# An attention-and-FFT kernel on one core: the order of every operation, the PSUM banks and the filler matmuls from tables instead of a scheduler

## The chip, the cores and the metric

One core of a Trainium2 chip. The metric is the time of one execution on the device in microseconds (us). Each run also records the span of the core (first to last instruction, about 1.8 us less than the metric) and the mean granted clock of TensorE (PE), 1.000 being full speed. A few more words: a PSUM bank is where a matmul of this program puts its result (`psA`, `psB`, `pvb` and `bg` below); a fall is a stretch in the middle of the kernel in which the granted clock is half of full (0.50 from 192.1 to 202.3 us in the profile of before); the head is the time until the first exponentials run at their regular pace, the tail what follows the last of them. Comparisons are between runs of the same call on the same chip where this is said.

A word on states: a run is called slow if it lies over 1.5% above the fastest of its kernel.

## The reference

A sigmoid gate mixes two branches of the same input x (2048 tokens, 448 features, bf16): attention with 16 heads of 28, and a filter in the frequency domain.

```python
def reference(A_x, A_wqkv, A_wo, B_x, B_w_r, B_w_i, gate_w):
    x = A_x
    g = _sigmoid((x * gate_w).sum(-1, keepdims=True))
    a = _A_ref(x, A_wqkv, A_wo)      # softmax(q k^T / sqrt(28)) v, then @ wo
    b = _B_ref(x, B_w_r, B_w_i)      # irfft2(rfft2(x) * (w_r + 1j * w_i))
    return g * a + (1 - g) * b
```

## The kernel before

The kernel describes 3123 operations, each with engine, duration, dependencies and a priority key. A list scheduler on the host puts them in order; the program then keeps that order on each engine. The work in the steady state is a chain of *score steps*: PE computes the scores of three 128x512 tiles into `psA`, or of two into `psB`, in turn; ScalarE (ACT) exponentiates them into `ring`; PE multiplies the exponentials with the values into `pvb`. A further share of exponentials is made on VectorE (DVE) from scores in one of two `bg` banks. Everything of the FFT branch is squeezed in between, also through the two `bg` banks.

The profile prints rows*columns with each: 128*128 for a projection, 32*128 for a score. A head has 28 features, padded to 32, so a score uses 32 rows, and the tiles of one step sit on different row groups; they run side by side (in the profile of before, three take 0.40 us together at 186.99, two 0.39 at 185.90, and a lone one 0.37 at 186.13):

```python
            def fm(st=st, slot=slot):
                for i in range(2):
                    for e, (n, kt, s) in enumerate(st):            # 2 or 3 tiles
                        ...
                            self.mm(slot[:, e, o:o + w], self.k[g][32 * s:32 * s + 32, ...],
                                    self.q[g][32 * s:32 * s + 32, ...], True, True,
                                    tile_position=(32 * s, 0))     # 32 rows of the array
            m = sc.op("PE", 0.23, fm, deps, -1000 + i * .001, 0.0, "row", name="score")
```

The scheduler already had fillers, matmuls of zeros with no purpose but to keep PE active. It decided on them by PE's *busy time* in the last 3.4 us:

```python
HAMW, HAMF = 3.4, 0.6838
...
        def share(t):
            a = t - HAMW
            while pebusy and pebusy[0][1] <= a:
                pebusy.pop(0)
            return sum(e - max(s, a) for s, e in pebusy) / HAMW

        def fill(t):
            ...
            if n < 96 or (share(t) >= HAMF and not head):
                return False
            ...
            o = Op("PE", n / 2400.0, lambda: self.filler(target, n), (), 0.0, 0.0, "col", ...)
```

## Time and profile before

| | before |
|---|---|
| time, 3 runs (4 with the later one) | 414.34, 415.25, 417.07 (415.83) us |
| profiled execution | 417.67 us, span 415.9, clock 0.973 |
| ACT busy / PE busy | 94% / 95% of the span |
| exponentials of three banks | 170, start to start 2.23 to 2.24 us where nothing disturbs |
| same, summed over what exceeds 2.24 | 16.7 us |

How to read it: ACT's sequence of exponentials is the spine (52% of the chain that ended last). As long as each exponential of three banks starts 2.24 us after the last one, nothing else in the kernel matters. So the useful question is not who is busy, but where that interval grows, and what was late there. The lines themselves stand in the prediction.

### The profile page before, as it was taken

What the parts mean: (1) busy time and instruction counts of PE and PEld (TensorE: products, weight loads), DVE (VectorE), ACT (ScalarE), POOL (GpSimd) and SP (SyncE); (2) the same over time, 40 slices, a digit from 0 to 9 for tenths busy, and PEclk for the clock granted to TensorE, in tenths of its full rate; (3) what the DMA queues carried; (4) which work ended last, traced back from release to release, by engine and by line L of the source; (5) the groups of instructions that cost most, each with busy time, mean ns of one, the idle gap of its engine ahead of it and who ended that gap; (6) DMA issues with size and microseconds to landing.
All of it is one profiled execution on the core that took longest, in us unless ns stands there. A gap on an engine that the chain in (4) does not pass through costs nothing.

```text
span 415.9 us, 12556 instructions
## 1 busy us (share of the span) xinstructions
PE 393.7 (95%) x5361; PEld 150.2 (36%) x5361; DVE 365.4 (88%) x629; ACT 392.0 (94%) x358; POOL 45.7 (11%) x95
## 2 busy tenths in 40 slices
PE   6998999999999999999999999999999999999995
PEld 4543333333433333234342332423334333333333
DVE  5758989888799999998699998798999989999965
ACT  4899999999999999998898998999999999999992
POOL 5400501001040000001041000000500000010000
PEclk9999999999999999997798996999999999999999
DMA  8500010001032310300103000231401200010102
GB/s 221 141 2 3 2 41 5 2 2 51 25 86 64 103 45 2 82 4 6 43 2 85 2 3 9 58 116 38 119 13 55 78 28 2 13 32 7 37 26 78
DMA packets 26548, 18.00 MB, mean 43 GB/s; under 512 B 10704, under 2 KB 24956, under 8 KB 26492
## 3 DMA queue, kind: packets, MB, share of 16 engines
q1 hardware_dynamic: 25660, 16.94, 14.9%
q8 instruction: 42, 0.69, 0.7%
q10 hardware_dynamic: 832, 0.26, 0.3%
q14 instruction: 14, 0.11, 0.1%
HBM read 11.31 MB, written 1.84 MB: 32 GB/s over the span
## 4 chain that ended last, share of the span: by engine, by line
ACT 53%; PE 28%; DVE 10%; issue 7%; DMA 2%; ACTq 0%; DVEq 0%
ACT ring L1620 52%; PE bg L908 11%; PE pvb L908 7%; PE psA L908 5%; PE psB L908 4%; DVE y L1574 3%; DVE pd L1584 2%; DMA U<-Y 1%; DMA U<-in_A_wqkv_dram 1%; DVE xtok L2003 1%; DVE k L1306 1%; DVE xtok L1316 0%; DVE pvs L1733 0%; DVE q L1306 0%; DVE xtok L2037 0%
## 5 line engine op out<-in xcount | busy, mean ns | idle before, releaser
L1620 ACT ACTIVATE ring<-psA 128x1536 bf16<-128x1536 f32 x170 | 260.9, 1535 | 6.4 <-PE psA L908 3.1
L1620 ACT ACTIVATE ring<-psB 128x1024 bf16<-128x1024 f32 (+1 forms) x170 | 188.0, 1106 | 3.8 <-PE psB L908 2.7
L1574 DVE TENSOR_SCALAR y<-bg 128x512 uint16<-128x512 f32 x176 | 117.3, 682 | 10.7 <-PE bg L908 10.0
L1584 DVE TENSOR_SCALAR pd<-y 128x2048 uint16<-128x2048 uint16 x176 | 118.6, 693 | 0.8
L908 PEld LDWEIGHTS <-k 32*128 32x128 bf16 (+1 forms) x1064 | 40.7, 91 | 125.8 <-issue 121.2
L908 PE MATMUL pvb<-ring,vw 128*32 128x512 bf16 (+1 forms) x872 | 78.0, 386 | 0.7 <-DVE pvs L1733 0.4
L908 PE MATMUL psA<-q,k 32*128 32x512 bf16 (+1 forms) x525 | 68.4, 383 | 5.1 <-ACT ring L1620 3.8
L908 PE MATMUL bg<-q,k 32*128 32x512 bf16 x176 | 65.2, 383 | 4.2 <-DVE Y L1958 1.6
L908 PE MATMUL psB<-q,k 32*128 32x512 bf16 (+1 forms) x347 | 67.5, 385 | 1.6 <-ACT ring L1620 1.4
L908 PE MATMUL pvb<-pd,vd 128*32 128x512 bf16 x704 | 64.5, 391 | 1.2 <-DVE pd L1584 0.8
L908 PEld LDWEIGHTS <-vw 128*32 128x32 bf16 x872 | 20.9, 95 | 33.3 <-issue 29.2
L908 PEld LDWEIGHTS <-vd 128*32 128x32 bf16 x704 | 18.4, 95 | 27.7 <-issue 22.9
L1478 POOL TENSOR_SCALAR vd<-vf 128x348 bf16<-128x348 f32 x16 | 20.6, 1290 | 60.7 <-DVE vf L1467 22.4
L1738 POOL CAST rhl<-rr 128x16 bf16<-128x16 f32 x15 | 6.0, 399 | 188.4 <-DVE rr L1737 188.4
L908 PEld LDWEIGHTS <-xT 128*128 128x128 bf16 (+3 forms) x512 | 21.2, 99 | 12.7 <-issue 9.6
L1958 DVE CAST Y<-bg 128x450 bf16<-128x450 f32 x32 | 19.6, 618 | 2.5 <-PE bg L908 1.2
L908 PE MATMUL bg<-xT,wpk 128*32 128x512 bf16 (+2 forms) x244 | 18.7, 389 | 0.0
L908 PE MATMUL bg<-xT,wpq 128*32 128x512 bf16 (+1 forms) x240 | 18.0, 383 | 0.2 <-DVE k L1306 0.2
L908 PE MATMUL bg<-Bd,xT 128*32 128x450 bf16 (+1 forms) x256 | 17.3, 356 | 0.0
L908 PE MATMUL bg<-wo,q 128*32 128x448 bf16 x236 | 16.4, 355 | 0.0
L908 PE MATMUL bg<-Bd,xtok 113*32 113x448 bf16 x240 | 16.0, 355 | 0.0
L1306 DVE TENSOR_SCALAR k<-bg 128x512 bf16<-128x512 f32 x15 | 10.3, 687 | 5.6 <-PE bg L908 5.4
(130 smaller groups left out, 316.6 us busy)
## 6 DMA issues: line engine op xcount, KB each, us to landing
U<-Y SPq DMA_DIRECT2D x32, 112.5 KB
CR<-cRB SPq DMA_DIRECT2D x8, 256.0 KB
out_dram<-U SPq DMA_DIRECT2D x14, 112.0 KB
CR<-cCS SPq DMA_DIRECT2D x8, 192.0 KB
xtok<-in_A_x_dram SPq DMA_DIRECT2D x3, 448.0 KB
xT<-escr SPq DMA_DIRECT2D x2, 512.0 KB
Wg<-in_B_w_r_dram SPq DMA_DIRECT2D x8, 112.5 KB
Wg<-in_B_w_i_dram SPq DMA_DIRECT2D x8, 112.5 KB
```

The lines of the kernel that those rows point to most:

```text
L908: self.pin(self.nc.tensor.matmul(out, lhsT=lhsT, rhs=rhs, start=start, stop=stop, **kw))
L1306: self.pin(nc.vector.tensor_scalar(out=dst, in0=self.bgi(it), scalar1=SQ, scalar2=None, op0=ALU.mult))
L1478: self.pin(nc.gpsimd.tensor_scalar(out=self.vd[g][:, f, :, :, 0:DH + 1], in0=self.vf[:], scalar1=PHGAIN[f], scalar2=None, op0=ALU.mult))
L1574: self.pin(nc.vector.tensor_scalar(out=ys[:, s, :], in0=self.bgi(it), scalar1=127 * UNITS, scalar2=0.0, op0=ALU.add, op1=ALU.max))
L1584: self.pin(nc.vector.tensor_scalar(out=fl(pds).bitcast(U16), in0=fl(ys), scalar1=float(PHASE[f]), scalar2=0.25, op0=ALU.add, op1=ALU.mult))
L1620: self.pin(nc.scalar.activation(out=self.ring[:, u0:u0 + len(st), :], in_=slot[:, 0:len(st), :], func=ACT.Exp, scale=LN2 / UNITS))
L1738: b = self.pool(0.3, lambda: self.pin(nc.gpsimd.tensor_copy(out=rhl[:, 0, :], in_=rr[:])), (a,), kk)
L1958: self.pin(nc.vector.tensor_copy(out=y[:], in_=self.bgi(it)[:, 0:F2]))
L2003: self.pin(nc.vector.tensor_tensor(out=t4.rearrange("p (a b) f -> p a b f", a=2), in0=free_dims(self.bgi(it), [[0, 2], [F, 2], [1, F]]), i ...
```

## The change

The intent, from the code: the order of every operation and the bank of every user of the two `bg` banks come from tables that were searched beforehand, so the scheduler goes. Fillers are in a table, too. The code also gives each PE operation a weight `util`, by which a score counts 0.23 per tile and not 1; this program sets it and never reads it, so that the search which made the table used it is my inference.

```diff
-HAMW, HAMF = 3.4, 0.6838
+HAMW, HAMF = 3.4, 0.6803
...
-KOFF = ( ...                        # 280 lines of priority offsets (cut)
+ORDER = (
+    119, 1, 0, 2, 7, 3, 12, 22, 94, 4, 21, 13, 32, 6, 10, 20, 14, 27, 5, 91, 8, 25, 11, 130, 2690, 19, 98, 18, 96,
+    ...                             # 3123 numbers (cut)
+FILLS = (                           # position, columns, target
+    (117, 192, 0), (126, 256, 1), (144, 256, 0), (144, 160, 0), (545, 128, 8), (834, 256, 8), (969, 256, 8),
+    ...                             # 51 entries (cut)
+BANKS = (
+    "0100011110110011010011111111111000011101010100101111010110011000100101100010101100011110010100110001"
+    ...
-    def run(self, nbg_tiles, dunits, dfree):      # the list scheduler (cut)
+    def run(self):
+        ...
+        for p, i in enumerate(ORDER):
+            while j < len(FILLS) and FILLS[j][0] == p:
+                n, t = FILLS[j][1:]
+                ...                  # a filler of n columns into bank t
+            o = self.ops[i]
+            assert all(d in done for d in o.deps)
+            done.add(o)
+            order.append(o)
...
+            m.util = 0.23 * len(st)                # a score of len(st) tiles
```

## The prediction

> **What bounds the kernel now.** I read the shares of the engines and the slices first, then the chain that ended last, then what ScalarE (ACT) waited for, then stretches of 4 us, then single instructions.

> The page of the kernel before (busy time by engine, the slices, the chain):

> ```profile
> span 415.9 us, 12556 instructions
> PE 393.7 (95%) x5361; PEld 150.2 (36%) x5361; DVE 365.4 (88%) x629; ACT 392.0 (94%) x358; POOL 45.7 (11%) x95
> ...
> PEclk9999999999999999997798996999999999999999
> ...
> ACT 53%; PE 28%; DVE 10%; issue 7%; DMA 2%; ACTq 0%; DVEq 0%
> ```

> ACT is 94% busy and more than half of the chain is its exponential (ring). PE looks equally full. The clock row is the odd one: five slices between 190 and 260 us ran below full clock. Which waits of ACT are real (waits of ACT alone):

> ```profile
> ACT t L1832 <- PE psA L908: 5.0, 1, 5.0
> ACT ring L1620 <- PE psA L908: 3.1, 5, 1.2
> ACT ring L1620 <- PE psB L908: 3.1, 5, 0.9
> ACT ring L1620 <- PE bg L908: 2.4, 5, 0.8
> ```

> The 5.0 is the tail. The exponential waits only for PE. Where: stretches of 4 us (busy us of each engine, then granted clock):

> ```profile
> 184.00:188.00 4.00, 3.69 (x56) 1.34 (x51) 4.00 (x8) 4.00 (x5) 0.00 (x0) 1.00 0.02 6
> 188.00:192.00 4.00, 3.24 (x37) 0.98 (x33) 4.00 (x7) 4.00 (x5) 1.17 (x2) 1.00 0.02 7
> 192.00:196.00 4.00, 3.93 (x34) 1.87 (x31) 3.40 (x7) 3.33 (x4) 0.75 (x2) 0.51 0.02 3
> 196.00:200.00 4.00, 4.00 (x37) 2.01 (x38) 1.74 (x3) 2.48 (x3) 0.00 (x0) 0.50 0.39 98
> 200.00:204.00 4.00, 4.00 (x49) 1.09 (x41) 1.90 (x3) 3.02 (x3) 0.00 (x0) 0.71 0.05 15
> ```

> A thin stretch on PE (37 matmuls, where 56 is usual) is followed by half clock for about 10 us, and ACT loses its full use there. The same around 219 us in the timelines of ACT and of PE:

> ```profile
> 214.27 1.48 ACT L1620 ACTIVATE ring<-psA 128x1536 bf16<-128x1536 f32 x1
> 216.51 1.51 ACT L1620 ACTIVATE ring<-psA 128x1536 bf16<-128x1536 f32 x1
> 218.74 1.53 ACT L1620 ACTIVATE ring<-psA 128x1536 bf16<-128x1536 f32 x1
> 221.99 1.45 ACT L1620 ACTIVATE ring<-psA 128x1536 bf16<-128x1536 f32 x1
> ```
> ```profile
> 218.60 0.37 PE L908 MATMUL bg<-q,k 32*128 32x512 bf16 x1
> 218.90 0.40 PE L908 MATMUL pvb<-ring,vw 128*32 128x512 bf16 x4
> 219.42 0.62 PE L908 MATMUL pvb<-pd,vd 128*32 128x512 bf16 x4
> 219.80 0.67 PE L908 MATMUL pvb<-ring,vw 128*32 128x512 bf16 x4
> 220.40 0.60 PE L908 MATMUL psB<-q,k 32*128 32x512 bf16 x2
> ```

> Starts of one exponential of three banks to the next: 2.23 or 2.24 us undisturbed, then 3.25. The same shape of matmul goes from 0.40 to 0.62 us near 219.4.

> From the first exponential of three banks (9.97) to the last (405.22) ACT takes 395.25 us for 169 intervals; at 2.24 each that is 378.6. The excess of 16.7 us I split by interval:
> - clock: 192.20 to 202.99 is 3 intervals, 10.79 - 6.72 = 4.07; 218.74 to 224.84 is 2, 6.10 - 4.48 = 1.62; 254.32 to 261.07 is 2, 6.75 - 4.48 = 2.27. Together **7.96 us**.
> - head, 9.97 to 18.50, 3 intervals: 1.81.
> - two long intervals at full clock: from 91.39 (3.46) and from 288.13 (3.23): 1.22 + 0.99 = 2.21.
> - the rest, 4.7, lies in many small ones: short exponentials of the weights w in the same queue, and waits of 0.1 to 0.3.

> [...] the clock falls near 192.15, 219.45 and 253.6, which are 8.0 and 10.0 windows apart, and the low stretches last about 3, 1 and 2 windows. [...] between 188 and 192 PE was busy 3.24 of 4 us, and no idle of PE there exceeded 0.45 us. [...] Counting every matmul as its columns[...] times the share of rows and of columns of the array that it uses, the whole run uses 0.61 of the array, but the windows ahead of the three falls only 0.40, 0.30 and 0.36. The lowest windows on that grid that did not fall were 0.38 to 0.39. So the limit appears to lie between 0.36 and 0.40, my boundaries being sure to 0.2 us; this is my estimate. A score of two or three 32-row tiles uses 2/4 or 3/4 of the array for its time, and a lone score into bg 1/4: thin stretches consist of these.

> **The change, part by part.**
> 1. *Host code.* The scheduler becomes a table. No instruction comes of that. Both programs have the same 3123 operations with the same work; ACT's order is nearly untouched (18 of 361 moved), so the sum of ACT's work stays.
> 2. *Fillers.* 24 become 51; each is four loads and four matmuls of zeros, so PE has 216 instruction rows more. By their columns they take 2.25 us before and 4.57 after: +2.3 us of array time. PE has 22 us of idle in the span, and they are put where PE has little to do; on the path I count 0.3.
> 3. *Order.* I cut each PE order at its scores and took windows of three score steps (3 x 1.12 = 3.36 us at the undisturbed pace). Of 325 windows beyond the head, before has 13 under 0.40 of array use, 5 under 0.35, minimum 0.30. After has 1 under 0.40 (0.394), none under 0.35. The mean is nearly equal (0.64 and 0.65): work was levelled, not added. [...] most of the 7.96 us goes: I count -7.7, leaving 0.3 for one chance in ten or so of a fall of 2 to 3 us.
> 4. *The long pairs.* PE's own work from one score of three tiles to the next (scores into bg taken as concurrent) had one case over 2.24 us: 3.10 at steps 72 and 73, which is the 1.22 us lost at 91.39. After, the largest is 2.47, at step 306. So -1.2 + 0.25, about -0.9.
> 5. *More mode changes.* Changes between row-tiled and column-tiled matmuls on PE go from 649 to 692. At an estimated 0.1 us (the difference between PE's idle of about 0.2 us in such places and none within a mode) that is 4 us of PE's slack; on the path I count 0.5.
> 6. *Banks.* 181 of 361 users of the two bg banks change bank. An item then waits for another reader, but both banks are read by the same DVE: 0 in the mean.
> 7. *The head.* PE has 53 operations before its first score where it had 46, which would start ACT some 0.5 us later; fewer stand between later scores (the fifth step has 1.41 us of work where it had 2.40, and 18.50 is just where ACT waited 1.2 us). I set both against each other: 0. The DMA order changes much: the bulk of wv moves from the 5th issue of the SyncE queue to the 23rd. By sizes some 3.4 MB stand before it, and the stretch from 0 to 13 us moved 236 GB/s, 3.07 MB, with 300 and more near its end, so it lands at about 15 us (estimate); its first user ran at 15.72. Just in time.

> Sum for the span: 415.9 - 7.7 - 0.9 + 0.3 + 0.5 = 408.1. The profiled execution took 417.67 as the metric has it, 1.77 more than its span, so 409.9. The timed runs (median 415.25) were faster than the profiled one, but they carry falls of the clock as well: with none, the profiled one would be at 409.7. I also give the 0.99 lost at 288 an even chance to vanish: **409.4 us**, 1.4% less.

> **Rivals.**
> - *The clock is not what it seems.* If the falls came by something else than array use, such as the DMA bursts, the new order would keep them: 414 to 417. Against: DMA is at 0.02 before the fall at 192, and all three falls follow thin windows. For: windows at 0.38 and 0.39 did not fall, so the limit is not seen sharply.
> - *PE becomes the bound.* The fillers and mode changes make 6 us more of PE time against 22 us idle. If they land next to scores, ACT waits 0.1 more at many of the 170 pairs, up to 5 us: 412 to 414. Against: apart from one pair no pair of steps holds more than 2.1 us of PE work.
> - *The head pays.* If wv or the weights behind it land 2 us late, the in-order PE queue holds the next score back: 411 to 412.
> - *More comes back.* If levelling removes the small waits as well (4.7 us in many places), 406 to 407.

> **Range and chances.** The centre needs the clock gain and nothing worse; both the second and third rival are one-sided upward, the fourth reaches 406.5. Range 406.8 to 412.8. Faster by over 2% means under 406.9: only if the small waits go too, 0.11. Slower by over 2% needs over 423.5, for which nothing in the profile stands: 0.01. Within 2%: 0.88.

> **What would show it.** Right: a clock row of nines, mean granted clock near 1.0 outside the last slice, no stretch where the matmul of 0.40 us becomes 0.61; ACT's 3.25 to 4.00 intervals gone; intervals of 2.24 unchanged; PE busy time up in count by 108 matmuls, but its idle near 20 us. Step 4: no interval of 3.4 us near the step of 91 us. Step 7: the fourth exponential of three banks near 18 us, no wait for wv. Wrong: a clock below 1.0 in any slice but the last; an interval of ACT stretched to 2.4 and more at many places with PE named (rival two); ACT waiting over 2 us before 20 us, PE held by a DMA (rival three).

The sum: 415.9 - 7.7 - 0.9 + 0.3 + 0.5 = 408.1 for the span, and 409.4 for the time. What is under the -7.7 is the count of stretches under 0.40 (13 before, 1 after); that they bring the falls was the estimate from three falls. The "windows" are stretches of 3.41 us: in the clock records of the trace of before all seven changes lie a whole number of 3.413 us apart (55, 3, 5, 1, 9, 2 and 45). Columns are counted at the kernel's own 2400 per us (the trace of e4 has 448 columns every 0.189 us, 2370 per us). The 0.1 us for a change of mode is in the trace of before, too: between 30 and 185 us, where a score (32*128) follows a column-tiled matmul (128*32) or the reverse, PE starts the second 0.10 us later than the columns of the first would have it (median of 238 places).

## More of the kernel before

At the very start 14 matmuls of zeros run before any data is there:

```python
        for i in range(14):
            self.pe(256, lambda: self.mm(self.psA[:, 2, 0:256], self.zero[:, 0:P], self.zero[:], True, True),
                    (ms["zero"],), K0 + i * .01, dur=0.214)
```

## The result, and the profile after

After: 410.46, 411.44, 411.45 and 412.0 us, median **411.44**; before in the same rounds 414.34, 415.25, 415.83 and 417.07, median 415.54. Ratios in this text are the mean time of one kernel's fast runs over that of the other's of the same rounds, so not quite the ratio of the medians: here 0.9897, with a 95% interval of 0.9859 to 0.9935. That is 1% faster, within the 2% that counts as the same, and inside the predicted range, but 2 us above the predicted 409.4.

The page of the kernel after (span, busy time, granted clock in 40 slices, shares of the chain):

```profile
span 409.6 us, 12755 instructions
...
PE 392.5 (96%) x5469; PEld 152.3 (37%) x5469; DVE 365.9 (89%) x629; ACT 389.8 (95%) x358; POOL 41.9 (10%) x95
...
PEclk9999999999999999999999999999999999999999
...
ACT 53%; PE 34%; issue 8%; DVE 2%; POOL 1%; DMA 1%; ACTq 0%; DVEq 0%; POOLq 0%
```

The row of the clock has only nines: the four low slices of before (7, 7, 8 and 6; the prediction says five) are gone. What ACT waited for in the kernel after (us in total, times, longest):

```profile
ACT t L1498 <- PE psA L572: 5.2, 1, 5.2
ACT wpq L691 <- POOL wpq L671: 2.8, 1, 2.8
ACT ring L1286 <- PE psB L572: 2.5, 3, 1.9
...
ACT ring L1286 <- PE psA L572: 0.4, 1, 0.4
```

In the kernel before, exponentials waited 8.6 us in 15 pieces for `psA`, `psB` and `bg`. Now it is 2.9 us in 4 pieces, and 1.9 of that is one wait, that of the very first exponential. The stretches of 4 us that held the first fall of the clock, in the kernel after (busy us of each engine, granted clock, share of the DMA engines, GB/s):

```profile
188.00:192.00 4.00, 3.91 (x56) 1.39 (x52) 4.00 (x7) 4.00 (x5) 0.00 (x0) 1.00 0.03 6
192.00:196.00 4.00, 3.75 (x58) 2.43 (x51) 4.00 (x8) 4.00 (x4) 0.00 (x0) 1.00 0.00 0
196.00:200.00 4.00, 4.00 (x61) 1.48 (x62) 3.97 (x7) 4.00 (x5) 0.00 (x0) 1.00 0.34 87
```

From 188 to 192 PE started 37 matmuls before and starts 56 now; its busy time was 3.24 us and is 3.91. The clock stays at 1.00 and ACT stays full.

The balance over the span, by starts of the exponentials of three banks (excess means time over 2.24 us per interval):

| part | before | after | difference |
|---|---|---|---|
| until the first one starts | 9.97 | 13.72 | +3.75 |
| excess, first 20 us | 1.88 | 0.54 | -1.34 |
| excess, 20 to 190 us | 3.39 | 2.67 | -0.72 |
| excess, 190 to 265 us (the falls) | 8.50 | 0.87 | -7.63 |
| excess, after 265 us | 2.92 | 2.14 | -0.78 |
| from the last one to the end | 10.68 | 11.10 | +0.42 |
| span | 415.9 | 409.6 | -6.3 |

The rows of excess are rounded separately and agree with the spans to 0.05 us. So 9.1 us were gained between 20 us and the last exponential, and about 2.4 lost at the head. These are two single executions, and that of before was an unusually slow one; between the medians of the timed runs the gain is 4.1 us. Where? First the exponentials in ACT's timeline, before:

```profile
9.97 1.45 ACT L1620 ACTIVATE ring<-psA 128x1536 bf16<-128x1536 f32 x1 [0.43 <-PE psB L908]
...
18.50 1.45 ACT L1620 ACTIVATE ring<-psA 128x1536 bf16<-128x1536 f32 x1 [1.20 <-PE psA L908]
```

and after:

```profile
13.72 1.45 ACT L1286 ACTIVATE ring<-psA 128x1536 bf16<-128x1536 f32 x1 [1.89 <-PE psB L572]
...
20.98 1.49 ACT L1286 ACTIVATE ring<-psA 128x1536 bf16<-128x1536 f32 x1
```

The fourth is 2.5 us late, and so is the eleventh (36.95 against 34.46). PE's timeline in the head, before:

```profile
6.83 0.60 PE L908 MATMUL psA<-xT,wpk 128*128 128x256 bf16 x4
```

and after:

```profile
4.53 0.84 PE L572 MATMUL psA<-zero 128*128 128x256 bf16 x3
7.47 0.40 PE L572 MATMUL psB<-xT,wpq 128*128 128x256 bf16 x1 [2.10 <-ACT wpq L688]
7.65 1.06 PE L572 MATMUL psA<-xT,wpk 128*128 128x256 bf16 x4
```

The same four matmuls took 0.60 us before and take 1.06 after. They keep that pace until about 12.5 us. PE is at half clock there, although the row of the clock shows a nine in these slices: in the packed trace of this run the first record of the clock begins at 12.7 us, where the clock rises (at 4.3 us in the kernel before), and the row and the mean count the time ahead of it as full. Reading durations of one shape is the surer way. Beside this, PE stood idle from 5.4 to 7.5 us: only ten of the 14 matmuls of zeros come before the projections in the new order (two of the other four run at 11.92 and 15.72 us, behind the projections, which waited 2.10 us for the weights), and a 448 KB load moved ahead of a part of the weights.

### The profile page after: what moved, and what is told of

It reads as the page before. It is cut to its first block, busy times and chain, and to the rows that moved or that the text cites. A ratio compares the mean times of both kernels' runs of the same rounds, so it can differ in the third digit from the quotient of the medians.

```text
span 409.6 us, 12755 instructions
## 1 busy us (share of the span) xinstructions
PE 392.5 (96%) x5469; PEld 152.3 (37%) x5469; DVE 365.9 (89%) x629; ACT 389.8 (95%) x358; POOL 41.9 (10%) x95
## 4 chain that ended last, share of the span: by engine, by line
ACT 53%; PE 34%; issue 8%; DVE 2%; POOL 1%; DMA 1%; ACTq 0%; DVEq 0%; POOLq 0%
ACT ring L1286 53%; PE bg L572 14%; PE pvb L572 9%; PE psA L572 6%; PE psB L572 5%; DVE y L1239 1%; DMA CR<-cRB 1%; PE bg L581 0%; POOL wpq L671 0%; POOL vd L875 0%; POOL wo L880 0%; DVE pd L1249 0%; ACT w L1068 0%; ACT t L1498 0%; DVE pvs L1399 0%
## 5 line engine op out<-in xcount | busy, mean ns | idle before, releaser
L1286 ACT ACTIVATE ring<-psA 128x1536 bf16<-128x1536 f32 x170 | 266.1, 1566 | 2.7 <-PE psB L572 1.9
L1286 ACT ACTIVATE ring<-psB 128x1024 bf16<-128x1024 f32 (+1 forms) x170 | 193.2, 1136 | 0.6 <-PE psB L572 0.6
L572 PEld LDWEIGHTS <-k 32*128 32x128 bf16 (+1 forms) x1064 | 44.0, 91 | 116.9 <-issue 110.3
L572 PE MATMUL pvb<-ring,vw 128*32 128x512 bf16 (+1 forms) x872 | 75.4, 377 | 0.3 <-DVE pvs L1399 0.2
L572 PE MATMUL pvb<-pd,vd 128*32 128x512 bf16 x704 | 63.2, 384 | 0.0
L572 PEld LDWEIGHTS <-vd 128*32 128x32 bf16 x704 | 16.7, 94 | 27.6 <-issue 23.8
L1404 POOL CAST rhl<-rr 128x16 bf16<-128x16 f32 x15 | 4.0, 267 | 223.9 <-DVE rr L1403 223.9
L572 PEld LDWEIGHTS <-xT 128*128 128x128 bf16 (+3 forms) x512 | 19.3, 96 | 12.7 <-issue 10.1
L1142 POOL TENSOR_SCALAR vd<-vf 128x348 bf16<-128x348 f32 x16 | 19.5, 1222 | 33.4 <-DVE vf L1131 32.6
L572 PE MATMUL bg<-wo,q 128*32 128x448 bf16 x236 | 16.7, 355 | 0.0
L572 PE MATMUL bg<-X,R 128*32 128x225 bf16 (+1 forms) x288 | 14.3, 294 | 0.0
```

Source lines behind the costliest of these rows:

```text
L572: self.pin(self.nc.tensor.matmul(out, lhsT=lhsT, rhs=rhs, start=start, stop=stop, **kw))
L1142: self.pin(nc.gpsimd.tensor_scalar(out=self.vd[g][:, f, :, :, 0:DH + 1], in0=self.vf[:], scalar1=PHGAIN[f], scalar2=None, op0=ALU.mult))
L1286: self.pin(nc.scalar.activation(out=self.ring[:, u0:u0 + len(st), :], in_=slot[:, 0:len(st), :], func=ACT.Exp, scale=LN2 / UNITS))
L1404: b = self.pool(0.3, lambda: self.pin(nc.gpsimd.tensor_copy(out=rhl[:, 0, :], in_=rr[:])), (a,), kk)
```

## The experiments

Their labels e1 to e11 follow the order in which they ran.

The theories after the result. *One:* the falls in the middle come from windows in which too few **rows** of the array are active, and the new order and fillers remove them. Rival: PE's busy time or its idle gaps decide. *Two:* the head is late because the clock has not risen yet. Rival: it is late because data land late and more work stands before the first score.

### Without the fillers (e1), and fillers on a quarter of the rows (e2)

```diff
 FILLS = (
-    ... 47 entries beyond the tenth score step
+    # only the first four, in the head
```

> The kernel after without its 47 fillers beyond the tenth score step; order and banks as they are. Counted from the order, the three-step windows under 0.40 of array use go from 1 to 4 (minimum 0.28), where before had 13 and fell 3 times. Theory (order does most, the fillers close the last holes): 0 to 2 falls of the clock in the profile, near steps 243 to 245 or 263 if any, mean granted clock 0.98 to 1.00, 411 to 414 us. Rival (the fillers carry the gain): three or more falls, clock under 0.98, 414 to 417 us. Rival (fillers only cost PE time): faster than after by 0.5 us or more at a clock of 1.00.

```diff
-    def filler(self, bank, n):
+    def filler(self, bank, n, quarter):          # quarter: beyond the head
+        r = 32 if quarter else P
...
-            self.mc(self.bgt[bank][:, 0:n], self.zero[:, 0:P], self.zero[:, 0:n], True, True)
+            self.mc(self.bgt[bank][:, 0:n], self.zero[0:r, 0:P], self.zero[0:r, 0:n], True, True)
```

> The same 47 fillers kept, each as long as before (same columns, same four column tiles), but on 32 rows in place of 128: a quarter of the array. Theory (the clock follows the share of the array in use): falls where the run without fillers has them, time within 1 us of it. Rival (the clock follows PE's busy time, whatever the share): as the kernel after, 411.4 us, clock 0.994 to 1.00. If the run without fillers shows no fall, this one cannot tell the two apart.

Measured: e1 had 410.44, 411.65, 415.38 and 417.16 us, with clocks of 0.997, 0.993, 0.981 and 0.982; ratio to before 0.9971 (0.9889 to 1.0052). e2 had 411.36 to 413.7, median 412.92, with clocks of 0.998 to 1.000 in all four; ratio 0.9977 (0.9921 to 1.0032). The kernel before, on the same chip, had a median of 414.47, at clocks of 0.976 to 0.994.

What follows: without fillers two of four runs fell by some 5 us; the other two are as fast as the changed kernel. In the profiled run of e1, which did not fall, the excess over 2.24 us is 6.21; in the changed kernel it is 6.22. So the 47 fillers cost nothing on the path, and the order alone does not seem enough: two of four runs fell, against three of 32 with all the fillers (counted below), which points that way and does not settle it. e2 is inconclusive: by theory one its fillers should have helped less, yet no run fell. Its three runs without a profile took 412.4 to 413.7 us at clocks of 0.998 to 1.000, up to 2 us more than the changed kernel; no trace shows where. From its trace I count 3.2 us of possible starts of windows of 3.41 us under 0.40 of the array (0.93 with full fillers, 4.99 without any), so four runs were too few to tell.

### What the clock follows: PE alone (e4)

A program with nothing but matmuls (and some copies on ACT to make PE wait), its result wrong:

```diff
+        def rows(pattern, reps):       # k tiles of 32 rows at a time
+            for r in range(reps):
+                for k in pattern:
+                    for s_ in range(k):
+                        self.mm(banks[s_][:, 0:N], x[32 * s_:32 * s_ + 32, 1, 0:P],
+                                x[32 * s_:32 * s_ + 32, 0, 0:N], True, True, tile_position=(32 * s_, 0))
+        def cols(k, reps): ...         # k tiles of 128 rows x 32 columns
+        def duty(n, reps): ...         # n full matmuls, then wait for a copy of ACT
+        full(80); rows([1], 140); full(80); rows([1, 1, 1, 2], 35); full(80); rows([1, 2], 70); ...
```

> Not the reference's computation (it copies its input out, wrong on purpose): PE alone, in stretches of 26 us or so with 15 us of full-array matmuls between. Row tiles of 32 rows, one at a time (0.25 of the array), patterns of mean 1.25, 1.5, 1.75, 2 and 3 tiles; column tiles one and two; full-array matmuls with waits for an activation between groups of 2, 3, 4 and 6; full-array matmuls of zeros. Theory (weighted use, limit between 0.36 and 0.40): 1.00 clock at 3 tiles, at 2 tiles (0.50) if they really overlap, and with zeros; half clock for most of the stretches at 0.25 to 0.31; the waits: half clock where columns streamed are under 0.36 of the time. Rival (busy time): no fall in any stretch of tiles, since PE has no gaps there; only the groups with waits fall.

Measured, stretches of 5 us (busy us and count of PE, of its weight loads, ACT, POOL; then the clock). One row tile; pattern of 1.75 row tiles; one column tile; full matmuls in pairs, and in threes:

```profile
65.00:70.00 5.00, 5.00 (x15) 1.85 (x13) 0.00 (x0) 0.00 (x0) 0.50 0.00 0
...
235.00:240.00 5.00, 5.00 (x49) 2.50 (x47) 0.00 (x0) 0.00 (x0) 1.00 0.00 0
...
365.00:370.00 5.00, 5.00 (x28) 2.59 (x27) 0.00 (x0) 0.00 (x0) 1.00 0.00 0
440.00:445.00 5.00, 2.85 (x7) 0.87 (x7) 1.65 (x4) 0.00 (x0) 0.50 0.00 0
475.00:480.00 5.00, 2.60 (x12) 1.09 (x12) 1.91 (x4) 0.00 (x0) 1.00 0.00 0
```

| load, coming from full clock | share of rows x time | clock |
|---|---|---|
| 1 row tile, no pause | 0.25 | falls to 0.50 |
| 1.25 row tiles in the mean | 0.31 | falls to 0.50 |
| 1.5 row tiles in the mean | 0.375 | falls to 0.50 |
| 1.75; 2 row tiles | 0.44; 0.50 | 1.00 |
| 1 column tile (128 rows, 32 columns) | 1.0 (of the array 0.25) | 1.00 |
| full, 2 per 1.17 us | 0.32 | falls to 0.50 |
| full, 3 per 1.42 us | 0.395 | 1.00 for 12 us, then falls |
| full, 4 per 1.6 us | 0.47 | 1.00 |

The loads that the fence leaves out: 1.25 and 1.5 row tiles had 0.50 at 110 to 115 and 170 to 175 us, two row tiles and full groups of four 1.00 at 270 to 275 and 530 to 535. The shares of the full groups are worked out: so many matmuls of 448 columns, 0.187 us each by the kernel's own rate of 2400 columns per us (the trace has 0.189 from start to start), over the period; they are means, and a single window can hold more or less. The first line of the fence settles the rival: PE busy in 5.00 of 5.00 us, no idle at all, and half clock. The pairs in the fourth line show the clock already down. The third line, set against the first, shows which "use of the array" counted here: with all rows and a quarter of the columns the clock was 1.00, with all columns and a quarter of the rows 0.50. My prediction counted rows times columns; for scores, which use all columns (32*128), it is the same. In these means 0.375 fell, 0.395 held 12 us and then fell, and 0.44 held. That a limit lies near 0.40 is my estimate from these loads; the prediction's (between 0.36 and 0.40) was one from three falls.

### The old head before the new order (e3)

```diff
-ORDER = (119, 1, 0, 2, 7, 3, ...)
+ORDER = (... all that stood before the tenth score in the kernel before, in its order,
+         ... then the rest in the order of the table)
```

> Every operation ahead of the tenth score step in the order, banks and fillers of the kernel before, the rest in the order of after. Theory (after lost 2.5 us in its head: its 11th exponential of three banks starts at 36.95 where before has 34.46): the 11th starts at 34.2 to 35.0, span 406.5 to 407.8, 408.5 to 409.6 us, clock 0.99 to 1.00. Rival (the head's loss is bought back later, since PE has work left over from the head): 410.5 to 412 us with longer intervals between 35 and 100 us.

Measured: 408.74, 409.70 and 410.18 us at a clock of 1.000, and one run of 415.44 at 0.982; ratio of the fast runs 0.9892 (0.9814 to 0.997). But the profile shows that the reason was not the one I expected. The fourth exponential of three banks came at 20.33 us, not near 18.5, and the PE timeline says why:

```profile
6.70 1.06 PE L571 MATMUL psA<-xT,wpk 128*128 128x256 bf16 x4
```

This is the head of the kernel before, instruction for instruction, and this time its projections ran at half clock (1.06), where they had run at full clock (0.60) in the profile of before. The same head was cold again in e8 below (fourth exponential at 20.34). So a part of the 2.5 us between the two first profiles is luck of that execution of before, not a property of its order. That the clock can be late in either head made the rise of the clock the next question.

### More matmuls of zeros at the start (e6), earlier weights (e7)

With the changed kernel once more on the same chip (e5) as their measure.

> The changed kernel once more, unaltered, on the chip of the three runs that follow, so that they have something to be compared with. Both theories of the head expect what was seen: first exponential of three banks at 13.0 to 13.9 us, PE matmuls of 128x256 at 0.42 us until 12 us, clock row of nines, fast runs at 410.3 to 412.0.

```diff
-ORDER = (119, 1, 0, 2, 7, 3, 12, ...            # zeros' memset second on POOL
+ORDER = (7, 1, 0, 2, 3, 119, 12, ...            # first; all 14 zero matmuls before the projections
...
-            self.pe(256, lambda: self.mm(self.psA[:, 2, 0:256], self.zero[:, 0:P], self.zero[:], True, True),
+            self.pe(256, lambda n=(1, 1, 2, 2, 2, 1, 1, 2, 1, 2, 2, 1, 2, 1)[i]: [self.mm(...) for _ in range(n)],
```

> The changed kernel with all 14 warm-up matmuls of zeros ahead of the first projections, and 7 more of them, so that PE is never idle from about 1.1 to 7.4 us; nothing else moves but the memset of the zeros to the front of POOL. Theory A: the head is late because PE still runs at half clock from 7.5 to 12.6 us [...]. Then the single 128x256 matmul after 7.5 us takes 0.27 instead of 0.42, PE's work up to the first score takes 2.5 to 3 us less, the first exponential of three banks starts at 11.0 to 11.8 instead of 13.7, and the fast runs lie 1.5 to 2.5 us below those of the changed kernel of this call. Theory B: the head is late because the weights land late and the PE has more work before the first score; then the start stays at 13.0 to 13.7 and the time within 0.5 us.

```diff
-    ..., 22, 94, 4, 21, 13, 32, 6, 10, 20, 14, 27, 5, 91, ...
+    ..., 22, 4, 21, 13, 32, 6, 10, 20, 14, 27, 5, 94, 91, ...     # 94: 448 KB of xtok
```

> The run before, and in addition the 448 KB load of xtok goes behind the two loads that follow it in SyncE's queue. Theory: it is this load that delays the last piece of the q and k weights (landing 6.7 us, in the kernel before 5.75). Then the copy of 64x112 starts near 5.8, PE's projections near 6.6, the first exponential of three banks 0.8 us earlier than in the run before (10.2 to 11.0), and the time falls by 0.8 more. Against it: the transposes that need the moved load come later and give it back; then the fourth exponential is no earlier than in the run before.

Measured: e5 had 410.8, 411.11, 411.3 and 411.99 us (clock 0.994 to 0.999). e6 had 408.72, 409.29 and 409.45 (0.997 to 0.999), and one run of 415.14 at 0.982. e7 had 409.13, 409.29 and 409.31 (0.998 to 1.000), and one of 414.04 at 0.987. The ratios of fast runs to the kernel before (0.997 for e5 and e6, 0.9949 for e7, all intervals across 1) say little here: one run of before, 409.41 at a clock of 0.999, was so fast that its ordinary ones of 415.94 to 416.68 were labelled slow and left out, leaving mostly its faster ones.

e6 in PE's timeline:

```profile
4.57 2.66 PE L572 MATMUL psA<-zero 128*128 128x256 bf16 x12
...
7.18 0.60 PE L572 MATMUL psA<-xT,wpk 128*128 128x256 bf16 x4
```

The projections take 0.60 again. The first exponential of three banks starts at 11.32 us (13.13 in e5), the fourth at 18.55 (20.36), the eleventh at 34.52 (36.33). Runs without a fall gain 2.1 us (mean 409.15 against 411.3). That is in the range of theory A, but not all of it is the clock. The projections start at 7.07 us in e6, at 7.69 in e5 and at 7.47 in the first profile of the changed kernel, with the same loads in the same order: the last piece of the weights simply landed at different times (VectorE's copy of it starts at 6.23, 6.92 and 6.69 us). So I count from the first projection instead:

| head | clock | first projection | from there to the fourth exponential |
|---|---|---|---|
| before, its first profile | full | 6.62 | 11.88 |
| before's head, e3 and e8 | late | 6.32, 6.65 | 14.01, 13.69 |
| changed kernel, its first profile and e2 | late | 7.47, 7.44 | 13.51, 13.41 |
| changed kernel, e1 and e5 | late until 10.3; on and off | 7.24, 7.69 | 12.73, 12.67 |
| with more zeros, e6 and e7 | full | 7.07, 6.69 | 11.48, 11.48 |

This takes the 2.48 us between the two first profiles apart (fourth exponential 18.50 and 20.98): +0.85 for the landing of the weights (6.62 to 7.47), +2.03 for the clock (11.48 to 13.51), and -0.40 for the order itself (11.88 to 11.48, both at full clock). The last two are not quite clean: the changed kernel has two matmuls of zeros in this stretch (at 11.92 and 15.72 us, 0.21 and 0.12 us until the next start), and e6 has moved them ahead of it. So up to 0.3 of the 2.03 is theirs, and some 0.2 of the 0.40 belongs to e6 rather than to the changed order. Theory two holds for the larger part, and the rival for 0.85 of it; that more work before the first score makes the head late is not borne out.

In e7 the weights do land earlier (copy at 5.82) and the projections start 0.38 us earlier than in e6. The time of the runs does not follow beyond their scatter of some 0.3 us. The expected 0.8 us was not there: it is 0.38 in this pair of profiles, less than e5 and e6 differ without any change of the loads.

### When the clock rises (e9)

PE alone again; each phase starts at half clock and then runs a steady pattern without a pause:

```diff
+        full(80)
+        rows([1], 50); rows([1, 2, 2, 2], 28); full(80)
+        rows([1], 50); rows([2], 110);         full(80)
+        rows([1], 50); rows([2, 3], 55);       full(80)
+        rows([1], 50); rows([3], 110);         full(80)
+        ...                                     # [3, 4] and [4]
```

> PE alone, result wrong on purpose. Each phase first brings the clock down (50 matmuls on one 32-row tile, a quarter of the rows), then runs a steady pattern for about 30 us without a pause: 1.75, 2, 2.5, 3, 3.5 or 4 row tiles in the mean (0.44, 0.50, 0.63, 0.75, 0.88, 1.0 of the rows), then full matmuls. The earlier run of this kind showed that 0.44 holds a full clock that is already there. Theory A, one limit for both ways: the clock rises in every phase within two windows (7 us). Theory B, the clock rises only after a window that is used far more than the one that holds it, as the heads of the kernels suggest (a window with about 0.5 or 0.65 of PE time did not raise it, one with 0.9 did): it stays at 0.50 through the phases of 0.44, 0.50 and perhaps 0.63, and rises in those of 0.88 and 1.0.

Measured, late in the phases of 2, 2.5 and 3 row tiles:

```profile
135.00:140.00 5.00, 5.00 (x29) 1.91 (x26) 0.00 (x0) 0.50 0.00 0
205.00:210.00 5.00, 5.00 (x38) 1.93 (x35) 0.00 (x0) 0.50 0.01 3
270.00:275.00 5.00, 5.00 (x84) 2.54 (x81) 0.00 (x0) 1.00 0.00 0
```

At half clock a matmul of 448 columns follows the last one after 0.37 us, at full clock after 0.19 (e9, at 79.53 and 83.68 us). So in the middle of a kernel the same matmuls keep their rows in use for longer, and in the kernel before the clock returned after 10.24, 3.41 and 6.83 us; that the one brings about the other is argued, not tested.

### Fillers on the order of before (e8)

The converse of e1: the order and the banks of before, with 54 fillers of 256 columns added so that no window of three score steps is under 0.46.

```diff
-ORDER = (the changed order)
+ORDER = (the order of the kernel before)
+FILLS = (its 24 fillers and 54 more of 256 columns at its thin steps)
```

> The kernel before in its own order and banks, with 54 fillers of 256 columns added so that every window of three score steps uses at least 0.46 of the array (5.8 us of array time added). Theory A, that array use in rows decides the clock and the order matters only through it: no fall of the clock in any run (mean 0.99 to 1.00, against 0.976 to 0.994 of the kernel before), intervals of 3 to 4 us at 190 to 260 us gone, time 408 to 411 if fillers cost nothing on the path, up to 413 if each costs 0.05 to 0.1. Theory B, that the order itself (bank waits, mode changes) is what matters: falls stay in most runs, time 413 to 416.

Measured: 413.83, 415.25, 415.99 and 416.82 us, at clocks of 0.998, 0.994, 0.998 and 0.992; ratio to before 1.0071 (0.998 to 1.0162). The page and ACT's waits:

```profile
PEclk9999999999999999999999999999999999999999
```
```profile
ACT ring L1289 <- PE psA L575: 4.5, 9, 1.2
ACT ring L1289 <- PE psB L575: 1.0, 2, 0.5
```

No run had a clock under 0.992, where 13 of 16 of before had 0.987 or less, and yet nothing was gained. The excess over 2.24 us is 13.56 us; before has 16.69 - 7.96 = 8.73 without its three falls. Of the 4.8 us more, 0.3 lie in the first 20 us, where the clock was late; the other 4.5 are what the 54 fillers cost on balance, 0.08 us each. Nine exponentials wait for `psA`, 4.5 us in all, where the changed kernel has one wait of 0.4 (and before five, 3.1 us, its falls included). Counted on the grid of windows that the clock records of e8 give, windows with 0.37 to 0.39 of the array were left, so that none fell is in part luck. Theory A of the expectation holds for the clock, and its upper estimate of the cost (413) was too low. The 47 fillers of the table cost nothing where they stand; that this is because the order made room for them is the likely reading, since e8 differs in the number, size and places of its fillers, too.

### The best version again, and with more fillers (e10, e11)

e10 is e7 once more, with more runs. e11 adds seven fillers of 192 columns at the thinnest steps:

```diff
+    (1308, 192, 8), (1308, 192, 8), (1308, 192, 8), (1966, 192, 8), (1966, 192, 8), (2309, 192, 8), (2324, 192, 8),
```

> The version with 21 warm-up matmuls and the earlier weights again, as the control of the next run and to see how often its clock falls: 2 of the 8 runs of the two warm versions fell (0.982, 0.987). Runs without a fall 408.9 to 409.6; if a fall is a chance of about one in four, one or two of the six runs at 413 to 415.

> The same with 7 more fillers of 192 columns at the five thinnest score steps, so that no window of three steps is under 0.45 by the count of columns (three were under 0.43, the thinnest 0.394). If the remaining falls come from those windows, all six runs keep a mean clock of 0.994 and more and lie at 408.9 to 409.8; a cost of the fillers on the path would be at most 0.4. If they come from elsewhere, falls stay as frequent as in the control.

Measured: e10 408.67 to 410.43 us, median **408.87**, ratio 0.9917 (0.9854 to 0.9981); e11 408.47 to 409.46, median 408.89, ratio 0.9913 (0.9843 to 0.9983). The clock was 0.997 to 1.000 in all twelve runs. Before on that chip had a median of 414.81 over eight runs. Without a fall in the control, the seven fillers show neither use nor cost. Both versions beat the changed kernel by about 2.3 us (e5, same chip, earlier).

### What the runs of before say together

The 16 executions of the kernel before whose clock is known lie along a line, time = 408.4 + 388 x (1 - clock), with a scatter of 0.9 us (my fit). Thirteen of them had a clock of 0.987 or less; the luckiest, at 0.999, took 409.41 us. So without a fall the kernel before would be *faster* than the changed one (410.46 to 412.0 in eight runs at 0.994 to 1.000), and about equal to the version with the warm head (409.2 in the median of its twelve runs without a fall in e6, e7 and e10, two others having fallen). This rests on the fit and on one run, whose head is not known, and it does not speak against the order: in the balance above before wins only at the head and in the tail, and between 20 us and the last exponential the changed kernel is 1.2 us shorter even without the falls (9.13 - 7.96). By this, most of what the change buys is insurance: none of its eight runs fell.

## Why the prediction was right, point by point

- *Step 2, fillers on the path (+0.3).* Measured 0.0, by the excess with and without them (e1).
- *Step 3, the clock (-7.7).* Right in size: the excess from 190 to 265 us went from 8.50 to 0.87 us. Thin windows as the cause agree with e4 (0.375 of the rows fell, 0.44 held), but the order alone leaves enough of them for two runs of four to fall (e1), so step 3 probably needed the fillers of step 2, which the prediction priced and gave no credit for. The clock records of the traces, whole numbers of 3.413 us apart, give the windows, so the count can be made on them: ahead of the three falls of before 0.34, 0.31 and 0.36 of the array were in use (the prediction, with boundaries sure to 0.2 us, had 0.40, 0.30 and 0.36), while between 20 and 400 us no window of the changed kernel had less than 0.43. Before also has windows of 0.36 and 0.37 that did not fall, so the limit is not seen sharply here.
- *Step 4, the long pairs (-0.9).* The interval of 3.46 us at 91.39 is gone; the excess from 20 to 100 us fell by 0.8 (2.52 to 1.73). In e8, which keeps the order of before, the interval is there again (3.46 at 94.20), so the order removed it. The 0.99 us at 288.13, to which an even chance was given, is gone as well; the excess after 265 us fell by 0.8. But e8 has lost it too (2.23 at 287.55), so this gain is not shown to come from the order.
- *Step 5, mode changes (+0.5).* Nothing of it shows: no row of the balance between 20 us and the tail grew. I have no run of this alone; that it is 0 is read from the sum.
- *Step 6, banks (0).* No run separates it. Nothing in the waits contradicts it.
- *Step 7, the head (0).* **This step failed in size: +2.5 us**, by the fourth exponential (20.98 against 18.50) as by the eleventh. What it argued about the order, more operations before the first score and fewer between the next ones, was right: at equal clock the new order (with e6's zeros) is even 0.4 us faster to the fourth exponential. What it left out were the pace and the first weights: up to +2.03 us because PE ran the first 5 us of work at half clock (1.06 us for four matmuls that took 0.60), and +0.85 because the q and k weights landed later. The pace was taken from one profile of before, in which the clock happened to be up; in two other executions the same head took 1.8 to 2.1 us longer. The load that step 7 did watch, wv, was not a wait of the profile after.
- *The rest.* The tail is 0.4 us longer (11.10 against 10.68), which no step had.

With 2.5 for the head and 0.4 for the tail, less the fillers and mode changes that cost nothing (0.8) and the 0.8 after 265 us, the predicted sum of 408.1 for the span becomes 409.4; measured was 409.6. That the total came so near is in part luck: 1.6 us of costs and waits that were not there hid more than half of the 2.9 us missed at the head and in the tail. Of the rivals, "the head pays" was the true one in its size (411 to 412); late weights, the cause that it named, made 0.85 of it, the clock more. "The clock is not what it seems" was wrong in this profile: no fall was left, and in e4 PE, busy 5.00 of 5.00 us both times, had a clock of 0.50 with a quarter of the rows in use and 1.00 with all of them (in a quarter of the columns).

What stays open: three of the 32 runs with the full set of fillers and the new order (one each in e3, e6 and e7; the eight of the changed kernel and the twelve of e10 and e11 did not) still fell to 0.982 or 0.987. None of these was a profiled run, so where they fell is not known. The thinnest windows that I count in the traces of these kernels are 0.38 and 0.40 near 156 and 243 us, which is between the 0.375 that fell and the 0.44 that held in e4, but e10 had the same windows in six runs without a fall. Whether fillers of a quarter of the rows protect less (e2) is open as well.

## What to carry to other kernels

Before trusting PE's busy time, count for each window of 3.4 us (the low stretches of before lasted 10.24, 3.41 and 6.83 us by the clock records: 3, 1 and 2 windows) how many *rows* of the array are in use for how long: in e4 one row tile kept PE busy for 5.00 of 5.00 us at a clock of 0.50, and 0.44 of the rows, which held a full clock in e4, had not brought it back after about 40 us in e9. Judge fillers by where they stand, not by their number; 47 of them were free in one order, and 54 others cost 4.5 us in another. At the start of a kernel, keep PE active without a pause until real work arrives (first exponential at 11.32 us in e6, 13.13 in e5), and compare head timings only after looking at the duration of one shape (four projections took 0.60 us in some profiles here and 1.06 in others), because whether the clock is up by then varied from run to run.
